# Block attention with a routed expert layer: the load order of the second and third groups of four heads

## The chip, the cores and the metric

The kernel runs on one core of a Trainium2 chip. The metric is the device time of one execution in microseconds (us). Three runs of the kernel before gave 835.05, 835.87 and 836.78 us; their median is 835.87 us. The engines are named as in the profile: PE multiplies matrices, PEld loads its weights, DVE and ACT work on vectors, POOL is the general-purpose engine, and SP only starts transfers (DMAs).

## The reference

Two parts follow each other. The first is attention for 8 batches of 8 heads, 576 positions and 64 channels per head, with a mask in blocks of 64:

```python
scores = scale * np.matmul(q, k.transpose(0, 1, 3, 2))
scores = np.where(block_i >= block_j, scores, -1000000000.0)
attn = np.exp(scores - np.max(scores, axis=-1, keepdims=True))
attn = attn / (np.sum(attn, axis=-1, keepdims=True) + 1e-09)
return np.matmul(attn, v)
```

The second takes the 4608 rows of 512 channels that this gives, picks for each row one of 8 experts by the largest of 8 logits, runs the row through two matrices of that expert with a ReLU between, and scales the result. The change touches only the first tenth of the first part.

## The kernel before, in words

**Heads and units.** Attention goes by pairs of heads: pair p = 0, 1, 2, ... is two heads, four pairs make a batch. The rows of q and k are loaded for four heads at a time, a *unit*: unit 0 is pairs 0 and 1, unit 1 (the second four heads) pairs 2 and 3, unit 2 (the third four heads) pairs 4 and 5, unit 3 pairs 6 and 7, and so on to unit 15.

**What a unit needs before its scores.** For each of k and q: a load from memory (tile `nat`, 576 KB in float32, `fetch`, line 91); a split of every value into a float16 part and the float16 rest (tile `sp`, `split`: a copy on DVE in line 96, a subtraction on POOL in line 97); a transposing DMA to a tile `tr` (`turn`, line 102; i = 0 is k, i = 1 is q). The scores multiply q by k and by a second copy of k in which the two halves of the partitions, part and rest, have changed places: the tile `sw`, made from the transposed k by two DMAs (`swap`, lines 107 and 108; this is the exchange). Lines 319 and 320 are the two score matmuls, of k and of `sw`. The pool `ld` gives `nat` four buffers and `sp` two, the number of the pool, so unit 1's first split reuses the buffer from which unit 0's k is transposed.

**Rows of v.** After the work of pair p has been written out, `load_v` (lines 303 to 306) starts four DMAs, 352 KB together, that pair's v. They are needed two pairs later, when `values` multiplies them, from line 417 on (vma and vmb first, then va and vb in lines 430 and 434).

**The order of the work.** `weave_` (line 287) goes round over generators: in each round every one of them writes out its next piece of work, first the softmax of pair p, the transposes of the probabilities of pair p - 1 (`flip`) and the products with v of pair p - 2 (`values`), then the generators in the list `later`, among them the loads. The weave of pair 0 has 5 rounds, of a later pair 8. PE follows this order exactly; on the other engines and on the SP queue a scheduler orders the instructions by priority (the order of writing) and by its own estimate of when each is ready. Every engine and the SP queue then takes its list in order, and an instruction that waits holds up all that is behind it.

**The start.** `load_start` makes unit 0 by halves: pair 0's heads through PE, the heads of pair 1 through two transposing DMAs (line 178) and two exchanges (lines 184 and 185). It makes unit 1 as well, with `nxt = Load(1)`. Its work by rounds is: round 1 of pair 0, the two transposes and unit 1's two loads; round 2, pair 1's exchange and unit 1's split of k; round 3, the transpose of unit 1's k; round 5, its split of q, which is issued after a mark `last_max` (line 363); round 1 of pair 1, the transpose of q; round 2 of pair 1, the exchange.

**The later units.** `load_heads(u)` (line 114) joins `later` at pair 2u - 3: round 1 of that pair, the two loads; rounds 5 and 6 the splits; rounds 1 and 2 of the next pair, the transposes; round 6 of it the exchange. Unit 2's loads are thus written in round 1 of pair 1, ahead of unit 1's exchange, and pair 0's v ahead of unit 1's transpose of q.

**Others.** `constants()` is written after pair 1 and is issued behind the last subtraction of a split (`last_lo`): five DMAs from POOL that set up a table of 290 KB and small weights.

Of the kernel before, what the change touches and what calls it, by code (L numbers as in the profile page):

```python
# [8 lines left out]
F16 = mybir.dt.float16  # L9
# [11 lines left out]
P = 128  # L21
# [5 lines left out]
def block_attention_top1_moe(  # L27
# [11 lines left out]
    nc = tc.nc  # L39
    B, H, S, D = q.shape  # L40
# [25 lines left out]
    MAXR = MAXH * S // P  # L66
# [8 lines left out]
    ld = tc.alloc_tile_pool(name="ld", bufs=2)  # L75
# [4 lines left out]
    class Load:  # L80
# [3 lines left out]
            self.u = u  # L84
            self.nats, self.sps, self.res = [], [], []

        def fetch(self):
            b, h0, nh = units[self.u]
            for src in (k, q):
                nat = ld.tile([P, MAXR, D], F32, name="nat", bufs=4)  # L90
                nc.sync.dma_start(nat, src[b, h0:h0 + nh].rearrange("h s d -> (h s) d").rearrange("(n p) d -> p n d", p=P))
                self.nats.append(nat)

        def split(self, i, hi, lo):
            sp = ld.tile([P, MAXR, 2, D], F16, name="sp")
            hi(sp[:, :, 0, :], self.nats[i])  # L96
            last_lo[0] = lo.tensor_tensor(sp[:, :, 1, :], self.nats[i], sp[:, :, 0, :], ALU.subtract)  # L97
            self.sps.append(sp)
# [15 lines left out]
    def load_heads(u):  # L114

        x = Load(u)
        x.fetch()
        todo = (
            lambda: x.split(0, nc.vector.tensor_copy, nc.gpsimd), lambda: x.split(1, nc.vector.tensor_copy, nc.gpsimd),
            lambda: x.turn(0), lambda: x.turn(1), x.swap,  # L120
        )
        at = 0
        for t, do in zip((4, 5, 8, 9, 13), todo):
            while at < t:
                at += 1
                yield
            do()
        x.done()

    units = [(b, h0, 4) for b in range(B) for h0 in (0, 4)]  # L130
    loaded = {}
    last_max, last_lo, last_exp = [None], [None], [None]

    def load_start():


        nr = 2 * S // P
        half = 2 * S
        nats = [ld.tile([P, 2, nr, D], F32, name="nat", bufs=4) for i in range(2)]
        sps = [ld.tile([P, 2, nr, 2, D], F16, name="sp") for i in range(2)]  # L140
        trs = [sb.tile([P, MAXR, P], F16, name=f"tr{which}") for which in (1, 0)] + [sb.tile([P, MAXH * S], F16, name="sw")]
        kT, qT = (x.rearrange("c r p -> c (r p)") for x in trs[0:2])
        sw = trs[2]
        for i in range(2):
            for src, nat in zip((k, q), nats):
                nc.sync.dma_start(
                    nat[:, i], src[0, 2 * i:2 * i + 2].rearrange("h s d -> (h s) d").rearrange("(n p) d -> p n d", p=P),
                )

        def halves(i, which, hi, lo):  # L150
            nat, sp = nats[which][:, i], sps[which][:, i]
            hi(sp[:, :, 0, :], nat)
            lo.tensor_tensor(sp[:, :, 1, :], nat, sp[:, :, 0, :], ALU.subtract)

        halves(0, 0, nc.vector.tensor_copy, nc.vector)
        halves(0, 1, nc.scalar.copy, nc.vector)
        rest = ps_t.tile([P, 512], F32, name="ps_t").rearrange("p (a n) -> p a n", n=P)
        for i, (sp, tr) in enumerate(((sps[0], kT), (sps[1], qT), (sps[0], sw))):
            sp = sp[:, 0]
            tv = tr[:, 0:half].rearrange("c (r p) -> c r p", r=nr)  # L160
            ps = ps_s.tile([P, 2, 512], F32, name="ps_s").rearrange("p a (b n) -> p (a b) n", n=P)
            for r in range(nr):
                o = ps[:, r] if r < 8 else rest[:, i]
                if i == 2:
                    for c in range(2):
                        nc.tensor.matmul(o[64 * c:64 * c + 64], sp[:, r, 1 - c, :], ident16, start=True, stop=True)
                else:
                    nc.tensor.matmul(o, sp[:, r].rearrange("p c d -> p (c d)"), ident16, start=True, stop=True)
            nc.vector.tensor_copy(tv[:, 0:4], ps[:, 0:4])
            nc.scalar.copy(tv[:, 4:8], ps[:, 4:8])  # L170
            nc.vector.tensor_copy(tv[:, 8], rest[:, i])
        loaded[0] = (qT, kT, sw)
        for which in range(2):
            halves(1, which, nc.scalar.copy, nc.gpsimd)
        yield

        for which in range(2):
            nc.sync.dma_start_transpose(
                trs[which][:, nr:], sps[which][:, 1].rearrange("p r c d -> p (r c d)")
            )  # L180
        nxt = Load(1)
        nxt.fetch()
        yield
        nc.sync.dma_start(sw[0:64, half:], kT[64:128, half:])
        nc.sync.dma_start(sw[64:128, half:], kT[0:64, half:])
        nxt.split(0, nc.vector.tensor_copy, nc.gpsimd)
        yield
        nxt.turn(0)
        yield
        yield  # L190
        with tc.issue_after(last_max[0].ins):
            nxt.split(1, nc.vector.tensor_copy, nc.gpsimd)
        yield
        nxt.turn(1)
        yield
        nxt.swap()
        nxt.done()

    with tc.high_priority(offset=3000):
        ident16 = const.tile([P, P], F16, name="ident16")  # L200
# [57 lines left out]
    with tc.manual_schedule(engines={mybir.EngineType.PE}), tc.high_priority(offset=2000):  # L258
        start = load_start()
        next(start)  # L260
# [504 lines left out]
    def split_w1(eng, b, src, c):  # L765
        sv = src.rearrange("p (g m) -> p g m", g=KF)
        split(eng, w1b[b][:, 0, c], w1b[b][:, 1, c].bitcast(BF16), sv)

    def split_w2(eng, b, src, c):
        sv = src.rearrange("p (g d) -> p g d", g=2)  # L770
        sl = slice(2 * c, 2 * c + 2)
        split(eng, w2b[b][:, 0, sl], w2b[b][:, 1, sl].bitcast(BF16), sv)
# [138 lines left out]


    loads = {2 * u - (4 if u == len(units) - 1 else 3): load_heads(u) for u in range(2, len(units))}
    loads[0] = start
    flips, prods = [], []
# [20 lines left out]
    for p in range(B * NP):  # L936
        b, hp = divmod(p, NP)
        u = p // 2
# [159 lines left out]
```

## Time and profile before

| what | value |
|---|---|
| median of three runs | 835.87 us |
| the profiled execution, its own time | 833.94 us |
| span of the trace in it | 831.9 us |
| mean granted clock of PE | 0.978 |
| PE busy | 777.9 us, 94% |
| DVE, ACT, POOL busy | 547.4, 517.4, 261.1 us |
| moved by DMAs | 151.21 MB, mean 182 GB/s |

The span runs from the first to the last instruction, so 2.0 us of the profiled execution lie outside it. In the rows, times count from the start of the span. A row of the timeline has the start, the duration, the engine, the line of the program, the operation, the tiles written and read, the number of instructions and, in brackets, the idle time before it and what ended it. For SP the duration is the time in which the queue was held by that DMA's start, not the time of the transfer. A granted clock of 1.00 is PE's upper level of 2.4 GHz, 0.50 the lower of 1.2 GHz. The share of the DMA engines can go over 1, because the packets of several transfers overlap.

### The profile page before, as it was taken

What the parts mean: (1) busy time and instruction counts of PE and PEld (TensorE: products, weight loads), DVE (VectorE), ACT (ScalarE), POOL (GpSimd) and SP (SyncE); (2) the same over time, 40 slices, a digit from 0 to 9 for tenths busy, and PEclk for the clock granted to TensorE, in tenths of its full rate; (3) what the DMA queues carried; (4) which work ended last, traced back from release to release, by engine and by line L of the source; (5) the groups of instructions that cost most, each with busy time, mean ns of one, the idle gap of its engine ahead of it and who ended that gap; (6) DMA issues with size and microseconds to landing.
All of it is one profiled execution on the core that took longest, in us unless ns stands there. A gap on an engine that the chain in (4) does not pass through costs nothing. (4 is left out here: it accounts for less than half of the span.)

```text
span 831.9 us, 17237 instructions
## 1 busy us (share of the span) xinstructions
PE 777.9 (94%) x6214; PEld 523.5 (63%) x6238; DVE 547.4 (66%) x1188; ACT 517.4 (62%) x1210; POOL 261.1 (31%) x233
## 2 busy tenths in 40 slices
PE   5599999999999999889996999999999999999995
PEld 3366666666676666555673766676656666776652
DVE  6467777878687777758561766786567656786540
ACT  4478786877778777666312855775555555775530
POOL 4322142424232243473236462223123222300001
PEclk9699999999999999999999999999999999999998
DMA  8999889799999899983158499685789968822611
GB/s 156 199 179 171 185 153 194 153 188 191 183 201 175 181 184 200 183 268 107 33 165 208 119 316 303 209 236 114 235 268 290 292 182 210 234 48 57 220 40 41
DMA packets 267053, 151.21 MB, mean 182 GB/s; under 512 B 235600, under 2 KB 235664, under 8 KB 266960
## 3 DMA queue, kind: packets, MB, share of 16 engines
q1 hardware_dynamic: 258688, 130.74, 68.6%
q0 software_dynamic: 8272, 19.29, 7.8%
q8 instruction: 51, 0.84, 0.4%
q14 instruction: 42, 0.34, 0.2%
HBM read 124.33 MB, written 19.73 MB: 173 GB/s over the span
## 5 line engine op out<-in xcount | busy, mean ns | idle before, releaser
L873 PEld LDWEIGHTS <-w1b 128*128 128x128 f16 (+1 forms) x2112 | 184.0, 98 | 26.5 <-issue 3.2
L873 PE MATMUL ps_s<-xt,w1b 128*128 128x256 f16 (+3 forms) x1824 | 182.1, 261 | 0.5 <-DVE w1b L763 0.4
L334 ACT ACTIVATE pt<-ps_s,nbs 128x448 f32<-128x448 f32 (+1 forms) x314 | 163.8, 531 | 23.9 <-DVE nbs L327 10.0
L900 PE MATMUL ps_t<-w2b,hh 128*128 128x512 f16 (+1 forms) x584 | 175.8, 379 | 2.3 <-ACT hh L881 2.3
L763 DVE TENSOR_TENSOR w2b<-w2f,w2b 128x1024 bf16<-128x1024 f32 x76 | 88.0, 1221 | 114.2 <-ACT w2b L762 114.2
L410 ACT COPY pT<-ps_t 128x512 f32<-128x512 f32 (+3 forms) x221 | 97.8, 463 | 74.1 <-PE ps_t L402 73.1
L402 PE MATMUL ps_t<-ident,pt 128*128 128x128 f32 (+1 forms) x800 | 133.0, 287 | 2.5 <-DVE xn L459 2.4
L900 PE MATMUL ps_t<-w2b,hl 128*128 128x512 f16 x304 | 115.2, 379 | 1.7 <-DVE hl L882 0.6
L97 POOL TENSOR_TENSOR sp<-nat,sp 128x1152 f16<-128x1152 f32 x30 | 71.2, 2375 | 145.1 <-DVE sp L96 111.2
L903 ACT ACTIVATE ys<-ps_t,ids 128x512 f32<-128x512 f32 x38 | 26.0, 688 | 137.7 <-PE ps_t L900 91.5
L319 PE MATMUL ps_s<-tr,tr 128*128 128x448 f16 (+1 forms) x378 | 99.6, 286 | 6.4 <-ACT pt L334 6.0
L900 PEld LDWEIGHTS <-hh 128*128 128x128 f16 x608 | 59.2, 98 | 69.2 <-ACT hh L881 2.8
L904 POOL DMA_INDIRECT out_dram<-ys,ids x38 | 43.4, 1143 | 185.2 <-ACT ys L903 134.5
L320 PE MATMUL ps_s<-sw,tr 128*128 128x448 f16 (+1 forms) x378 | 92.2, 286 | 9.4 <-DMA sw<-tr 9.4
L402 PEld LDWEIGHTS ps_t<-ident,pt 128*128 128x128 f32 (+1 forms) x800 | 87.8, 143 | 18.4 <-issue 5.5
L763 DVE TENSOR_TENSOR w1b<-w1f,w1b 128x1024 bf16<-128x1024 f32 x76 | 88.0, 1221 | 0.2 <-ACT w1b L762 0.2
L434 PE MATMUL ps_a<-pT,vb 128*64 128x512 f32 (+3 forms) x256 | 83.5, 450 | 0.0
L430 PE MATMUL ps_a<-pT,va 128*64 128x512 f32 (+3 forms) x256 | 83.5, 450 | 0.0
L372 DVE TENSOR_REDUCE nmx<-ps_s 128x2 f32<-128x896 f32 (+1 forms) x63 | 60.2, 956 | 32.7 <-PE ps_s L322 32.5
L762 ACT CAST w1b<-w1f 128x1024 f16<-128x1024 f32 x76 | 74.0, 1044 | 0.3 <-DMA w1f<-in_moe_w_dram 0.2
L762 ACT CAST w2b<-w2f 128x1024 f16<-128x1024 f32 x76 | 73.6, 1042 | 0.0
L736 POOL DMA_INDIRECT xg<-x_d,ids x38 | 55.3, 1455 | 53.5 <-DMA ids<-tab_d 20.6
(196 smaller groups left out, 1122.0 us busy)
## 6 DMA issues: line engine op xcount, KB each, us to landing
w1f<-in_moe_w_dram SPq DMA_DIRECT2D x76, 512.0 KB
w2f<-in_moe_w_dram SPq DMA_DIRECT2D x76, 512.0 KB
nat<-in_k_dram SPq DMA_DIRECT2D x15, 576.0 KB
nat<-in_q_dram SPq DMA_DIRECT2D x15, 576.0 KB
sw<-tr SPq DMA_DIRECT2D x30, 288.0 KB
x_d<-xn SPq DMA_DIRECT2D x32, 256.0 KB
va<-in_v_dram SPq DMA_DIRECT2D x32, 128.0 KB
vb<-in_v_dram SPq DMA_DIRECT2D x32, 128.0 KB
```

What stands on the lines that cost most here:

```text
L97: last_lo[0] = lo.tensor_tensor(sp[:, :, 1, :], self.nats[i], sp[:, :, 0, :], ALU.subtract)
L319: nc.tensor.matmul(ps_ap, qq, k1[ab][:, c0:c1], start=True, stop=False)
L320: nc.tensor.matmul(ps_ap, qq, k2[ab][:, c0:c1], start=False, stop=last)
L334: last_exp[0] = nc.scalar.activation(probs[t][0:r, ab * n:(ab + 1) * n], ap, AF.Exp, bias=nbs[0:r, t, ab:ab + 1], scale=SCALE, accum_out=s ...
L402: nc.tensor.transpose(ps[:, i, 0:rows], probs[t][0:rows, P * col:P * col + P], ident[0:rows, 0:rows])
L410: copies[next(nth)](pT[:, r:r + m, Q0[t]:Q0[t] + rows], ps[:, i:i + m, 0:rows])
L430: nc.tensor.matmul(pa[0:64, P * j:512], va[:, j, :], pT[:, 1 + 2 * j, 64 + P * j:576], start=False, stop=(j == 3),)
L434: nc.tensor.matmul(pa[64:128, P * j:512], vb[:, j, :], pT[:, 2 + 2 * j, 64 + P * j:576], start=False, stop=(j == 3),)
L762: nc.scalar.copy(hi, src)
L763: eng.tensor_tensor(lo, src, hi, ALU.subtract)
L873: nc.tensor.matmul(ph[:, f4].rearrange("p (h n) -> p h n", n=P), wv[:, cc, f, :], xv[:, cc], start=(k == 0), stop=(k == 3 * KD - 1))
L900: nc.tensor.matmul(py, hv[:, f, h], wv[:, f, :], start=(k == 0), stop=(k == 3 * KF - 1))
```

## The change: the diff

```diff
-        def fetch(self):
+        def fetch(self, *which):
             b, h0, nh = units[self.u]
-            for src in (k, q):
+            for src in [(k, q)[w] for w in which or (0, 1)]:
...
         def split(self, i, hi, lo):
-            sp = ld.tile([P, MAXR, 2, D], F16, name="sp")
+            sp = ld.tile([P, MAXR, 2, D], F16, name="sp", bufs=4)
...
     def load_heads(u):
 
         x = Load(u)
+        late = LATE if u == 2 else 0
+        for i in range(late):
+            yield
         x.fetch()
...
+    LATE = 4
...
-        sps = [ld.tile([P, 2, nr, 2, D], F16, name="sp") for i in range(2)]
+        sps = [ld.tile([P, 2, nr, 2, D], F16, name="sp", bufs=4) for i in range(2)]
...
+
+        nxt = Load(1)
+        nxt.fetch(0)
...
-        nxt = Load(1)
-        nxt.fetch()
+        nxt.fetch(1)
+        nxt.split(0, nc.vector.tensor_copy, nc.gpsimd)
         yield
         nc.sync.dma_start(sw[0:64, half:], kT[64:128, half:])
         nc.sync.dma_start(sw[64:128, half:], kT[0:64, half:])
-        nxt.split(0, nc.vector.tensor_copy, nc.gpsimd)
-        yield
         nxt.turn(0)
         yield
         yield
...
             nxt.split(1, nc.vector.tensor_copy, nc.gpsimd)
         yield
         nxt.turn(1)
-        yield
         nxt.swap()
         nxt.done()
+
 
```

Unit 1's work by rounds becomes: its load of k is written right behind unit 0's loads, ahead of pair 0; round 1 of pair 0, the load of q and the split of k; round 2, the transpose of k; round 4, the split of q; round 5, the transpose of q and the exchange. All of it is then written in pair 0's weave, ahead of pair 0's v and of pair 1. Unit 2 alone moves by four rounds: its loads to round 5 of pair 1, its splits to rounds 1 and 2 of pair 2, its transposes to rounds 5 and 6 of pair 2, and its exchange from round 6 of pair 2 to round 2 of pair 3, behind pair 2's v and behind the loads of unit 3, which stay in round 1 of pair 3. `sp` has four buffers. No instruction is added or taken away. Since `last_lo` is then unit 1's last subtraction when `constants()` is written, those five DMAs wait for that one and no longer for unit 2's.

## Rows read from the trace of the kernel before

**Rows 1.** Waits of PE, whole run: line, releaser: us in total, times, longest.

```profile
PE ps_s L320 <- DMA sw<-tr: 9.4, 2, 8.7
```

**Rows 2.** Timeline of PE: first scores of pairs 1 to 4, first of L417.

```profile
19.83 0.19 PE L319 MATMUL ps_s<-tr,tr 128*128 128x64 f16 x1
...
30.72 0.20 PE L319 MATMUL ps_s<-tr,tr 128*128 128x64 f16 x1
39.60 0.23 PE L320 MATMUL ps_s<-sw,tr 128*128 128x64 f16 x1 [8.68 <-DMA sw<-tr]
...
41.75 0.37 PE L417 MATMUL ps_t<-pT,vma 128*64 128x64 f32 x1
...
51.48 0.19 PE L319 MATMUL ps_s<-tr,tr 128*128 128x64 f16 x1
...
61.50 0.19 PE L319 MATMUL ps_s<-tr,tr 128*128 128x64 f16 x1
```

**Rows 3.** Timeline of the SP queue from 14 to 54 us.

```profile
14.57 0.59 SPq L185 DMA_DIRECT2D sw<-tr  x1
20.09 2.68 SPq L102 DMA_TRANSPOSE tr<-sp  x1
22.81 0.58 SPq L303 DMA_DIRECT2D va<-in_v_dram  x1
...
25.97 2.76 SPq L102 DMA_TRANSPOSE tr<-sp  x1
28.77 0.57 SPq L91 DMA_DIRECT2D nat<-in_k_dram  x1
...
31.54 2.35 SPq L107 DMA_DIRECT2D sw<-tr  x1
...
46.04 0.52 SPq L107 DMA_DIRECT2D sw<-tr  x1
...
51.61 1.64 SPq L91 DMA_DIRECT2D nat<-in_q_dram  x1
```

**Rows 4.** Stretches: length, busy us of PE, PEld, DVE, ACT, POOL, granted clock, DMA share, GB/s.

```profile
17.00:21.00 4.00, 1.85 (x16) 1.29 (x15) 3.97 (x7) 2.67 (x8) 2.61 (x2) 0.86 0.05 12
21.00:26.00 5.00, 4.54 (x19) 2.81 (x20) 2.99 (x12) 3.54 (x15) 2.12 (x1) 0.50 0.95 184
26.00:27.00 1.00, 1.00 (x7) 0.90 (x6) 0.62 (x1) 0.40 (x2) 0.00 (x0) 0.63 0.28 54
...
39.60:43.60 4.00, 4.00 (x27) 3.26 (x27) 1.68 (x8) 1.60 (x9) 4.00 (x6) 0.50 1.10 230
39.00:58.00 19.00, 18.40 (x142) 12.17 (x142) 11.35 (x34) 12.83 (x47) 4.92 (x6) 0.87 1.08 205
...
53.00:57.00 4.00, 4.00 (x38) 2.82 (x36) 2.77 (x8) 3.56 (x17) 0.00 (x0) 1.00 1.27 243
57.00:60.00 3.00, 3.00 (x25) 1.57 (x20) 2.14 (x7) 2.45 (x8) 1.92 (x1) 1.00 0.74 151
60.00:61.00 1.00, 1.00 (x11) 0.59 (x10) 0.65 (x2) 1.00 (x4) 0.46 (x1) 1.00 0.00 1
```

**Rows 5.** Timeline of DVE and POOL: the splits of units 1 and 2, the table.

```profile
16.81 0.75 DVE L96 CAST sp<-nat 128x1152 f16<-128x1152 f32 x1
...
18.49 2.19 DVE L96 CAST sp<-nat 128x1152 f16<-128x1152 f32 x1
...
34.17 0.76 DVE L96 CAST sp<-nat 128x1152 f16<-128x1152 f32 x1 [3.06 <-DMA nat<-in_k_dram]
37.49 0.76 DVE L96 CAST sp<-nat 128x1152 f16<-128x1152 f32 x1 [2.56 <-DMA nat<-in_q_dram]
...
17.70 2.37 POOL L97 TENSOR_TENSOR sp<-nat,sp 128x1152 f16<-128x1152 f32 x1 [6.82 <-DVE nbs L327]
20.75 2.36 POOL L97 TENSOR_TENSOR sp<-nat,sp 128x1152 f16<-128x1152 f32 x1 [0.69 <-DVE sp L96]
...
40.63 0.74 POOL L267 DMA_DIRECT2D tab_d<-tinit  x1
```

## The prediction

> **What bounds the kernel now.** I read the waits of PE first, since it is busy for 94% of the span. Over the whole run its largest releaser is the exchange, 9.4 us, of which one wait has 8.7 [rows 1]. The timeline of PE gives its place: the first score of pair 2 against k runs at 30.72, its partner against `sw` at 39.60, and PE stands for 8.68 us between [rows 2]. So pair 1 takes 10.89 us from its first score (19.83 to 30.72), pair 2 takes 20.76 with the wait, pair 3 takes 10.02 (51.48 to 61.50).
>
> The SP queue, read next, tells why the exchange is late. Unit 1's k is transposed at 20.09. Then come pair 0's v, the transpose of q at 25.97, unit 2's loads from 28.77, and at 31.54 at last the exchange [rows 3]. It does not need the transposed q, nor the v, nor the loads; it stands behind them. Its transfer also runs behind theirs: the DVE copy of unit 2's q starts at 37.49 as soon as that load has landed [rows 5], and PE is released 2.1 us later [rows 2].
>
> The stretches show the second thing to see: the DMA engines have little room here. Between 39 and 58 us they move 205 GB/s at a share of 1.08; they stand almost still from 17 to 21 (12 GB/s), when SP waits for unit 1's first split, dip from 26 to 27 (54 GB/s), and run dry only at 60 [rows 4]. Whatever is moved forward pushes something else back.
>
> **The change part by part.**
>
> *Removed: the wait of 8.68 us.* In the new order the exchange of unit 1 follows its two transposes with only those ahead. When can they go? SP is free for the transpose of k at 15.2 (14.57 + 0.59 [rows 3]). It needs the split. The copy took 0.75 us at 16.81 and the subtraction 2.37 us at 17.70 [rows 5]; no row shows when the load of k had landed. Bounds: the copy cannot come later than now by this edit, and if it goes one round up, into the softmax of the first rows, it is done some 2 to 4 us earlier. I take 3, a subtraction ending at 17 rather than 20.07, because the queue's transfers end at 17 in any case and nothing else wants the engines then [rows 4]. So the transpose of k moves from 21.3 (its transfers begin 1.2 us after 20.09) to about 17.7.
>
> The copy of q stands at 18.49 and took 2.19 us beside POOL's subtraction, against 0.75 for the same shape at other times; POOL began q at 20.75 and took 2.36 [rows 5]. With k's subtraction gone earlier I take the short value: the copy ends near 19.2, the subtraction near 21.6, and the transpose of q starts there instead of at 25.97. The bounds are 20.5 and 23.1 (20.75 + 2.36, nothing gained). It holds SP for 2.76 us; the exchange, with 2.1 us of transfer behind the transpose's, lands between 27.5 and 30.5. Pair 2 wants it at 30.72, or up to 1.5 us sooner if pairs 0 and 1 run shorter. The wait goes, or leaves less than 1 us.
>
> *Removed with it: a cold start.* PE is at the lower clock after the wait, 0.50 from 39.6 to 43.6 [rows 4]. From the release, pair 2 needs 11.88 us (39.60 to 51.48), pair 3 10.02 [rows 2], so 1.86 us are the clock. If nothing took their place, the two would give 8.68 + 1.86 = 10.54 us, and pair 4 would start at 50.96 instead of 61.50.
>
> *Moved back: pair 0's v.* Four DMAs now follow the exchange and are issued by 28. Line 417 first reads them 2.15 us after pair 2's restart at 39.60 [rows 2], so near 32. They have 352 KB, 1.7 us at 205 GB/s; cover 0 to 2 us, cost taken as nothing, up to 1 us if the exchange lands at 30.5.
>
> *Moved forward: the table and small weights of `constants()`.* POOL starts them at 40.63 [rows 5]; they move to behind q's subtraction, near 22. Some 0.3 MB, 1.6 us of transfer at 205 GB/s, can fall between the transposes and the exchange. They lie inside the margin just given, and leave a later stretch, so no cost in sum.
>
> *Moved back: unit 2, by four rounds.* This decides the size. In pair 2 DVE meets unit 2's copies in rounds 1 and 2, and everything behind a copy waits for its load. Before, both copies waited, 3.06 and 2.56 us [rows 5], while PE stood still anyway; that cover is gone. More, unit 2's exchange now stands behind unit 3's loads, just as unit 1's did behind unit 2's.
>
> Take the list of transfers from unit 1's transpose of k to the end of unit 3's loads. In both orders it has the same members, except that unit 2's exchange now comes last (it was issued at 46.04, ahead of unit 3's loads, whose second started at 51.61 [rows 3]). Before, the list ran from 21.3 to about 57.5: from 57 to 60 there were 453 KB, 352 of them pair 3's v, so 100 KB of loads were left at 57 [rows 4]. After: it begins 3.6 us earlier (17.7), has a new gap between the transposes of k and q, since v no longer fills the wait for q's split (17.7 + 2.7 = 20.4 to 22.8, 2.4 us), and loses the old gaps at 26 and 52, about 1.8 together. End: 57.5 - 3.6 + 2.4 - 1.8 = 54.5, and with 0.5 us for the landing unit 2's exchange is there at 55.0. Pair 4 would be ready at 50.96. So some 4 us come back, spread over DVE's waits for the loads of units 2 and 3 and PE's for this exchange; they are one delay, not to be added up, since all hang on the same list.
>
> *Sum.* Pair 4 starts at 55.0 instead of 61.50: 6.5 us. If the new waits are long enough to take PE to the lower clock, 1.86 us go again; between 0 and 1.86 I take 0.9. Gain 5.6 us. Ends: the list may end 2 us sooner or later by the bounds on the two splits and the gap, and the clock 0.9 either way, so 2.7 to 8.5. From 60 us on the engines run dry at times [rows 4], so the order behind is set by the rounds and moves along.
>
> *At nothing:* the argument of `fetch` (no instruction), the load of k written earlier (it is ahead of unit 0's transposes on SP already), and two more `sp` buffers, memory alone beside what they free.
>
> Against the profiled execution: 833.94 - 5.6 = 828.3. The median stood 1.93 above it, so 835.87 - 5.6 = 830.3.
>
> **The rivals.**
>
> *The queue keeps up.* Plain loads went at 243 GB/s from 53 to 57 against the mean of 205 [rows 4]. If the list went at 243, its 34.4 busy us (21.3 to 57.5 less 1.8) would shrink to 29.0, and from 17.7 with the gap of 2.4 it would end at 49.1; pair 4 would not wait. Then the gain is 10.5, with 0.7 more if the short copy of q also shortens pair 0: 835.87 - 11 = 824.9. Against it stand the transposes and the v, at 184 [rows 4]. A sentence for the page: the Trainium skill (DMA: Bandwidth & Descriptors, section on bandwidth) gives 341 GB/s for a load of 1 MB, which would make the same case more strongly; the rows here stay well under it.
>
> *The exchange is not ahead.* The scheduler decides the SP queue, not the writing alone. If unit 2's loads still go first, or unit 1's q is not split sooner, the wait stays: 835.9, no change. Against it: in the rows the queue follows the order of writing for v, transposes, loads and exchange.
>
> *Slower: the four rounds.* If unit 2's loads are held until round 5 of pair 1 in fact, and the engines are idle meanwhile, four rounds (5.0 us at 10.02 for eight) are added to the list: it ends at 62.5, the exchange lands at 63.0, pair 4 starts 1.5 us later than at 61.50, cold for 1.86 more: 835.87 + 3.4 = 839.3. It decides once unit 2's first load is issued 4 us or more after the present 28.77, with the engines standing idle between. For it: the rounds are counted in PE's time. Against it: by round 5 of pair 1 SP is still busy with v, so the queue should not be empty.
>
> **How the numbers follow.** A measurement of this kernel can tell about 0.2% from no change, 1.7 us. Chances: the forecast 0.58, the queue keeps up 0.23, not ahead 0.10, slower 0.09. The first two are faster by more than 1.7 us: 0.81; 0.10 the same, 0.09 slower. The forecast's own range is 835.87 less 8.5 and less 2.7, 827.4 to 833.2; to reach the first rival the low end goes to 824.3, and the high end to 834.2, the edge of no change.
>
> **What would show each step.** Right: no wait of PE on `sw` near 31; the two transposes of unit 1 and the exchange ahead of line 303 on SP; transfers from 17 or 18 us on; pair 2 starting at 29 to 31 at the full clock; waits of DVE line 96 in pairs 2 and 3, and unit 2's exchange issued behind unit 3's loads, with PE waiting for it at 52 to 56. Wrong: pair 4 starting at 51 with no wait (too little gain forecast), a wait at line 417 for v, or an idle stretch of the DMA engines before unit 2's loads.

## The result, and the profile after

The changed kernel took 841.41 us in the median of 7 runs (839.80 to 846.97), the kernel before 836.20 us in 7 runs beside them: a ratio of 1.0067, 95% interval 1.0041 to 1.0093. The change costs 5 us; 830.3 had been forecast, with 824.3 to 834.2 as the range. The profiled execution of the changed kernel took 841.41 us itself, with a span of 839.4 us. Two executions of later kernels, of 1003.53 and 1650.32 us, are slow ones and stand in no median or ratio below. In the changed kernel the lines up to 108 keep their numbers, and those behind are 3 to 7 higher: L319 and L320 are L324 and L325, L303 is L308, L417 is L422.

The waits of PE over the whole run come first again:

```profile
PE ps_s L325 <- DMA sw<-tr: 10.9, 4, 8.3
PE ps_t L422 <- DMA vma<-in_v_dram: 4.1, 2, 2.7
```

The exchange still costs PE 10.9 us, where it cost 9.4 [rows 1]. The timeline of PE shows that the long wait has only moved, from pair 2 to pair 4:

```profile
30.45 0.20 PE L324 MATMUL ps_s<-tr,tr 128*128 128x64 f16 x1 [1.21 <-DMA tr<-sp]
32.58 0.20 PE L325 MATMUL ps_s<-sw,tr 128*128 128x64 f16 x1 [1.93 <-DMA sw<-tr]
...
44.81 0.19 PE L324 MATMUL ps_s<-tr,tr 128*128 128x64 f16 x1
...
54.83 0.19 PE L324 MATMUL ps_s<-tr,tr 128*128 128x64 f16 x1
63.28 0.23 PE L325 MATMUL ps_s<-sw,tr 128*128 128x64 f16 x1 [8.26 <-DMA sw<-tr]
```

Pair 2 waits 1.21 + 1.93 us instead of 8.68 and starts 7 us sooner [rows 2]. But from its release at 32.58 to pair 3's first score at 44.81 it takes 12.23 us, where it took 11.88 with the lower clock before and pair 3 takes 10.02. Pair 4 stands from 55.0 to 63.28, later than its start at 61.50 before. The SP queue tells what is ahead of its exchange:

```profile
15.78 10.58 SPq L102 DMA_TRANSPOSE tr<-sp  x2
26.45 0.54 SPq L107 DMA_DIRECT2D sw<-tr  x1
27.68 1.01 SPq L308 DMA_DIRECT2D va<-in_v_dram  x1
...
31.54 0.59 SPq L91 DMA_DIRECT2D nat<-in_k_dram  x1
...
37.92 0.62 SPq L311 DMA_DIRECT2D vmb<-in_v_dram  x1
43.32 6.99 SPq L102 DMA_TRANSPOSE tr<-sp  x2
...
53.51 1.55 SPq L91 DMA_DIRECT2D nat<-in_q_dram  x1
55.18 2.63 SPq L107 DMA_DIRECT2D sw<-tr  x1
```

Unit 1's exchange is now ahead of v and of unit 2's loads, as planned. Between pair 1's v (issued by 38.54) and unit 2's transposes at 43.32 SP issues nothing, and unit 2's exchange stands at 55.18 behind unit 3's loads. The splits say why SP waits; they come from the timelines of DVE and POOL:

```profile
40.03 0.75 DVE L96 CAST sp<-nat 128x1152 f16<-128x1152 f32 x1
43.72 0.75 DVE L96 CAST sp<-nat 128x1152 f16<-128x1152 f32 x1
```

```profile
21.20 0.74 POOL L272 DMA_DIRECT2D tab_d<-tinit  x1
40.92 2.37 POOL L97 TENSOR_TENSOR sp<-nat,sp 128x1152 f16<-128x1152 f32 x1 [16.43 <-DVE nbs L332]
```

Unit 2's split of k begins at 40.03 and ends on POOL at 43.29; the transpose follows 0.03 us later. The two copies show no wait for a load, unlike before [rows 5]: they stand late in DVE's own list, k's behind the third group of pair 2's maxima (line 377 at 39.02), q's behind the last one (line 388 at 43.05). The stretches of 1 us give the DMA engines' side (columns as in [rows 4]):

```profile
24.00:25.00 1.00, 1.00 (x10) 0.72 (x9) 0.48 (x4) 0.98 (x3) 0.50 (x1) 1.00 1.08 69
25.00:26.00 1.00, 0.59 (x5) 0.28 (x4) 0.97 (x2) 1.00 (x6) 0.00 (x0) 1.00 2.09 50
...
35.00:36.00 1.00, 1.00 (x8) 1.00 (x5) 0.20 (x1) 0.66 (x5) 0.00 (x0) 0.50 1.22 202
...
40.00:41.00 1.00, 1.00 (x8) 0.16 (x4) 0.91 (x4) 0.57 (x3) 0.08 (x1) 1.00 0.08 13
41.00:42.00 1.00, 1.00 (x11) 0.72 (x10) 0.23 (x1) 1.00 (x3) 1.00 (x1) 1.00 0.00 0
...
44.00:45.00 1.00, 1.00 (x16) 0.82 (x13) 0.54 (x2) 0.77 (x3) 0.45 (x1) 1.00 0.47 95
...
64.00:65.00 1.00, 1.00 (x6) 0.69 (x5) 0.59 (x2) 0.00 (x0) 0.11 (x1) 0.50 1.20 233
```

Three things are to be read here. The engines stand still from 40 to 44.4. From 24 to 26, while what POOL has started from 21.20 on (the table and the small weights) is on its way, they are busy by their share (1.08 and 2.09) and move only 69 and 50 GB/s. And PE is at its lower clock after the new wait, as it was after the old one [rows 4], and at 34 to 37 after the short waits of pair 2 as well.

One measure compares all kernels below: the start of a pair's first maximum on DVE, the first thing done with its scores. The table, worked out from the timelines of DVE, gives it as the difference in us to the profile of before, whose pair 2 stands at 40.73, pair 4 at 62.57 and pair 5 at 72.64. Pairs count from 0; minus is sooner.

| kernel | 2 | 4 | 5 | 7 | 16 | 25 |
|---|---|---|---|---|---|---|
| before, second profile | +1.1 | +1.1 | +1.1 | +1.0 | +1.1 | +1.2 |
| changed | -7.5 | +1.8 | +3.5 | +3.5 | +5.2 | +5.1 |
| table late | -10.4 | -0.9 | +1.2 | +1.2 | +3.0 | +3.0 |
| copies sooner, again | -8.1 | 0.0 | +1.8 | +1.8 | +3.5 | +2.9 |
| both together | -10.3 | -1.7 | +0.7 | +0.7 | +4.3 | +4.2 |
| changed, a third time | -7.4 | +2.8 | +4.6 | +4.6 | +7.2 | +6.4 |
| exchange first | -8.1 | -6.4 | -6.0 | -5.7 | +5.4 | +4.3 |
| unit 3 later | -8.3 | -3.7 | -2.3 | -2.9 | +12.2 | +11.2 |
| no late | -9.2 | -5.1 | -3.5 | -2.7 | +10.3 | +9.4 |
| exchange order alone, again | -9.5 | -9.2 | -7.2 | -7.2 | +7.0 | +6.1 |
| four buffers, again | -3.5 | -3.0 | -3.0 | -3.0 | -3.9 | -3.7 |

The loss of the changed kernel is made at pairs 4 and 5: +3.5 there, of which 1.6 between the two pairs are put down to the lower clock. Other profiles of the same kernel have +4.6 and, below, +1.5 at pair 5. Another 1.7 us come by pair 16. Between pair 25 and the end of the span the difference goes from 5.1 to 7.5 us, about as far as the two profiles of before drift apart there (from 1.2 to 3.0 us at pair 30).

### The profile page after: what moved, and what is told of

Same layout as the page of the kernel before. It is cut to its first block, busy times and chain, and to the rows that moved or that the text cites. A ratio compares the mean times of both kernels' runs of the same rounds, so it can differ in the third digit from the quotient of the medians.

```text
span 839.4 us, 17223 instructions
## 1 busy us (share of the span) xinstructions
PE 781.1 (93%) x6214; PEld 524.9 (63%) x6238; DVE 545.4 (65%) x1188; ACT 517.9 (62%) x1210; POOL 262.9 (31%) x233
## 5 line engine op out<-in xcount | busy, mean ns | idle before, releaser
L324 PE MATMUL ps_s<-tr,tr 128*128 128x448 f16 (+1 forms) x378 | 100.2, 287 | 5.4 <-ACT pt L339 3.8
L909 POOL DMA_INDIRECT out_dram<-ys,ids x38 | 49.0, 1291 | 178.4 <-ACT ys L908 103.9
L325 PE MATMUL ps_s<-sw,tr 128*128 128x448 f16 (+1 forms) x378 | 92.5, 286 | 10.9 <-DMA sw<-tr 10.9
L388 DVE TENSOR_REDUCE nmx<-ps_s 128x1 f32<-128x576 f32 x64 | 48.3, 755 | 38.4 <-PE ps_s L327 37.6
```

Source lines behind the costliest of these rows:

```text
L324: nc.tensor.matmul(ps_ap, qq, k1[ab][:, c0:c1], start=True, stop=False)
L325: nc.tensor.matmul(ps_ap, qq, k2[ab][:, c0:c1], start=False, stop=last)
```

## The experiments

My theory after the result: unit 2's exchange is late by its place behind unit 3's loads, and that list of transfers ends 8 us later than forecast because the DMA engines stand still while unit 2 is split, and because the table's transfers run beside unit 1's transposes. The rivals: the four rounds delay the loads of unit 2, or the place in the queue is no matter.

**Exchange first.** The changed kernel, with unit 2's exchange written in the round of its transpose of q, ahead of pair 2's v and of unit 3's loads.

```diff
-        for t, do in zip((4, 5, 8, 9, 13), todo):
+        for t, do in zip((4, 5, 8, 9, 9 if u == 2 else 13), todo):
```

> Edit: in the changed kernel, unit 2's exchange is written right behind its transpose of q, so that it stands ahead of pair 2's v and of unit 3's loads. Theory A (order alone: pair 4 waits 8.3 us because the exchange stands behind the loads): the wait of PE on sw near 55 goes to under 1 us, the first max of pair 4 comes near 56 instead of 64.4, the time falls by about 10 us to 831. Rival B (the list of transfers is late as a whole, and DVE takes its copies in order): unit 3's loads now land later, near 57 and 59.5, the DVE copies of unit 3 hold up pair 3's last maxima and pair 4's first until 60 to 61; the wait on sw goes, but the time falls by only 3 to 4 us, to 837 or 838, about that of the kernel before.

Measured: 845.47 us, ratio 1.0133 [1.0091, 1.0174]. The exchange is issued at 50.58 and the wait is gone:

```profile
55.48 0.20 PE L325 MATMUL ps_s<-sw,tr 128*128 128x64 f16 x1 [0.37 <-DMA sw<-tr]
```

The place in the queue decides the wait; of 8.26 us, 0.37 are left. But the time is no better; neither expectation had one so long. The lead of 6 us holds to pair 7 and is lost from pair 8 to 16 (table). Moving this one DMA also changes the lists of the later batches, since the scheduler orders everything behind anew: PE's list differs from before's near 94, 141 and 186 us, where the transposes of a finished batch stand between the scores, and is the same there in the changed kernel. So this run shows what the wait hangs on, and not what it is worth.

**Table late.** The changed kernel with `constants()` written one pair later.

```diff
-    CP = 1
+    CP = 2
```

> Edit: in the changed kernel, constants() (the table of 290 KB and the small weights, five DMAs from POOL) is written after pair 2 and not after pair 1, so that it is issued behind unit 2's last subtraction and no longer at 21 us beside unit 1's transpose of q. Theory A (the table's DMAs slow that transpose; 69, 50 and 103 GB/s from 24 to 27 us): PE's waits at the start of pair 2, 1.2 and 1.9 us, shrink to under 1 us in all, pair 2 starts 2 to 3 us sooner; pair 4 gains at most as much, the time falls by 0 to 2 us. Rival B (the transpose of q is slow by itself): pair 2 still waits about 3 us, and the time stays at 841.

Measured: 843.22 us, ratio 1.0067 [1.0041, 1.0094]. SP's queue in this run:

```profile
15.23 8.16 SPq L102 DMA_TRANSPOSE tr<-sp  x2
```

The two transposes are done on SP 8.16 us after the first is issued, instead of 10.58. In the other profiles with the table at 21 to 22 us it is 9.4 to 10.2, in the other two with a late table 8.2 and 8.4; so the table beside unit 1 costs 1.1 to 2.4 us at that place. Pair 2 starts with a wait of 0.29 us and keeps the full clock (1.00 from 26 to 52), and unit 2's copy of k, behind the same maxima in DVE's list, starts at 35.10 instead of 40.03. The only list that differs from the changed kernel's is POOL's. Pair 4 comes 2.7 us sooner, and 2.2 of that are left at pair 16; but with the table at 41.94 a like hole appears at 45 to 47, and pair 4 still waits 9.43 us, until 60.55. The ratio is the one that the changed kernel had in its own comparison, so a gain in time is not shown.

**No late.** The changed kernel with unit 2 in its old rounds.

```diff
-    LATE = 4
+    LATE = 0
```

> Edit: LATE = 0 in the changed kernel, unit 2's loads, splits, transposes and exchange at their old rounds. On SP and DVE this gives the same order as the kernel with the exchange written first; only the table differs, which is issued behind unit 2's subtractions. Theory A (the four rounds are what loses): the exchange of unit 2 is ahead of unit 3's loads, no wait on sw at pair 4, and without the table at 21 us pair 2 starts 2 to 3 us sooner; 829 to 834, faster than the kernel before. Rival B (the copies of units 2 and 3 on DVE wait for their loads, whatever the rounds say): DVE waits of 5 us and more in pairs 2 and 3, pair 4's first max at 59 to 61, 834 to 838.

Measured: 844.07 us, ratio 1.0085 [1.0055, 1.0116]. Unit 2's loads are issued at 28.78, behind unit 1's exchange and pair 0's v as in the changed kernel, and its transposes at 42.17 (43.32 there). The run above, with a late table too but the late rounds, has the loads at 28.73 and the transposes at 38.39. So the late rounds hold back neither: the loads follow SP's queue, and the transposes wait for the split of k, whose copy starts at 38.88 here. The idle stretch before them is there with the old rounds too (0.02 and then 0.00 of the engines from 39 to 43). What the rounds do change is the place of the exchange, which is now ahead of unit 3's loads, and pair 4 waits 1.55 us for it (and 1.08 for the transposed q and k). Both expectations had a shorter time; the lead of 5.1 us at pair 4 goes as with exchange first, and PE's list differs from before's at the same three places.

**Buffers alone.** The kernel before with four split buffers in both places, and no other edit.

```diff
-            sp = ld.tile([P, MAXR, 2, D], F16, name="sp")
+            sp = ld.tile([P, MAXR, 2, D], F16, name="sp", bufs=4)
...
-        sps = [ld.tile([P, 2, nr, 2, D], F16, name="sp") for i in range(2)]
+        sps = [ld.tile([P, 2, nr, 2, D], F16, name="sp", bufs=4) for i in range(2)]
```

> Edit: the kernel before with four sp buffers, nothing else of the change. Theory A (the order of the queue holds the exchange back, not the buffers): unit 1's k is split and transposed some 4 to 5 us sooner, but its exchange still stands behind pair 0's v, the transpose of q and unit 2's loads; PE waits 6 to 8.7 us for it, the time stays within 2 us of the kernel before, 834 to 836. Rival B (the buffers by themselves cost time later on, by other places in memory or other orders): 838 or more.

Measured: 832.71 us, ratio 0.9958 [0.9932, 0.9985]: faster than before, by more than either expectation had. DVE's copy of unit 1's k starts at 11.60 instead of 16.81 [rows 5], its transpose at 15.26 instead of 20.09, the exchange at 27.88 instead of 31.54 [rows 3], and PE waits 7.28 us instead of 8.68. So the copy had been held by the buffer, not by its place in the order, and all lists but DVE's stay as they were.

**Copies sooner.** The changed kernel, with both of unit 2's copies one maximum sooner in DVE's list.

```diff
+            with tc.issue_after(copied[2, 0].ins) if b == 0 and hp == t == 2 else nullcontext():
...
+            with tc.issue_after(copied[2, 1].ins) if b == 0 and hp == 2 else nullcontext():
```

> Edit: in the changed kernel, unit 2's two copies stand sooner in DVE's list: k's behind pair 2's second maximum and no longer its third, q's behind the third and no longer the fourth. Nothing else moves in the SP queue. Theory A (the DMA engines stand idle from 40 to 44 us because these copies come late in DVE's list, and the whole list of transfers behind them is late by that): the transposes of unit 2 are issued from 41.7 and 44.2 us instead of 43.3 and 46.9, the exchange of unit 2 lands 2 to 3 us sooner, pair 4's first maximum comes at 61.5 to 62.5 instead of 64.4; the time falls by about 2 us. Rival B (the rate of the transfers alone decides, a gap here only moves the wait): pair 4's first maximum stays at 64 or later.

Measured: 858.45 us, ratio 0.9987 [0.9963, 1.0010], on a chip where the kernel before took 859.66. Its traces show stalls of about 4 to 5 us that the profile puts down to a releaser named remote, in every kernel on that chip; one of them lay in pair 2 of this profile, and the copies ran at 42.12 and 43.89, later than in the changed kernel. Inconclusive; repeated below.

**Exchange order alone.** The kernel before with four buffers, and unit 1's exchange written in the round of its transpose of q.

```diff
         nxt.turn(1)
-        yield
         nxt.swap()
         nxt.done()
+        yield
```

> Edit: the kernel before with four sp buffers and the exchange of unit 1 written in the round of its transpose of q, so that it is ahead of unit 2's loads on SP; pair 0's v stays ahead of the transpose of q, LATE is not there. Theory A (an earlier start is given back later, because the lists of DVE, ACT and SP that the scheduler then makes for the batches behind are worse ones, as when the exchange of unit 2 was put first): pair 2 starts near 30, pair 4's first maximum at 55 to 58, 4 to 6 us ahead of the kernel before until pair 7, then 2 to 3 us are lost on each unit up to pair 17; the time is 838 to 846. Rival B (what is lost later is the work of the change's other parts, the late unit 2 and the v behind the exchange): the lead stays, 829 to 832.

Measured on the same chip: 858.53 us, ratio 0.9969 [0.9941, 0.9996]. Pair 2 waits 0.82 us and pair 4 is 9.2 us ahead of the first profile of before, of which nothing is left by pair 12. Held against the kernel before on its own chip (next), which has the stalls too, the lead is 10.8 us at pair 4 and 4.6 at pair 12. What the stalls do to either was not separated, so this was repeated too.

**Changed and before, again,** on that chip, one run each, no edit.

> The changed kernel once more, for a second trace: how much of its distance to the kernel before comes in the same place. If the lists decide, pair 5 is again 3 to 4 us behind the kernel before, with PE's wait of about 8 us on unit 2's exchange; if it is scatter, that wait differs by more than 2 us.

> The kernel before once more, for a second trace: the scatter of its pairs 10 to 30. If the drift of 4 us that the changed kernel shows there against the first trace is scatter of the runs, this trace also differs from the first by 2 to 4 us there; if it is the lists, this trace stays within 1 us of the first.

Measured: 854.6 and 860.91 us. The waits come back as they were: 8.90 us at pair 4 in the changed kernel, 8.66 at pair 2 in the one before, and pair 5's first maximum is at 74.18 and 74.16. The changed kernel was expected 3 to 4 us behind there and is level, since unit 2's transposes were issued at 40.94 in this profile and its wait ended at 61.54. So the place of the loss comes back, its size does not. Behind pair 8 the stalls named remote come in; two single runs with such stalls tell nothing of a difference under 1%.

**Both together.** Copies sooner and the table late, on another chip, where the kernel before took 836.62 us.

```diff
-    CP = 1
+    CP = 2
...
+            with tc.issue_after(copied[2, 0].ins) if b == 0 and hp == t == 2 else nullcontext():
...
+            with tc.issue_after(copied[2, 1].ins) if b == 0 and hp == 2 else nullcontext():
```

> The changed kernel with two of its side effects taken out: the table's DMAs go one batch part later, and DVE's copies of the third four heads stand one and two maxima earlier in its list. Theory B (the forecast's list is right and only its two neglected terms, the idle gap from 40 to 44.4 and the table beside unit 1's transposes, spoil it): SP holds the two transposes of unit 1 for about 8.2 us instead of 10.6, the idle stretch before unit 2's transposes shrinks from 4.4 to under 2.5, and PE's wait at pair 4 ends at 56 to 59 instead of 63.28; pair 4's first maximum at -3 to -6 against before. Rival (the queue order alone decides, unit 2's exchange behind unit 3's loads): the wait still ends at 61 or later. Time: by Theory B 829 to 835 if the lead is kept; if later batches give it back as in the run with the exchange first, 835 to 843 with the lead at pair 4 all the same.

Measured: 840.51 us, ratio 1.0041 [1.0023, 1.0059]. PE at pair 4:

```profile
59.72 0.23 PE L325 MATMUL ps_s<-sw,tr 128*128 128x64 f16 x1 [7.54 <-DMA sw<-tr]
```

The exchange lands 3.6 us sooner than in the changed kernel (63.28), and 4.5 sooner than in the changed kernel on this chip (64.24, below). It was expected between 56 and 59, the rival had 61 or later; neither came. The transposes of unit 1 take 8.23 us on SP. The stretches show how much of the idle time is left, and the table's hole at its new place:

```profile
37.00:38.00 1.00, 0.44 (x3) 0.20 (x3) 1.00 (x3) 1.00 (x5) 1.00 (x1) 1.00 0.00 0
38.00:39.00 1.00, 1.00 (x10) 0.73 (x9) 1.00 (x1) 0.78 (x4) 0.52 (x1) 1.00 0.00 0
39.00:40.00 1.00, 1.00 (x12) 0.75 (x12) 1.00 (x3) 0.57 (x2) 0.79 (x1) 1.00 0.22 46
44.00:45.00 1.00, 1.00 (x14) 0.68 (x9) 0.21 (x1) 1.00 (x7) 0.83 (x2) 1.00 2.59 155
45.00:46.00 1.00, 1.00 (x10) 0.78 (x9) 0.80 (x1) 0.59 (x3) 0.00 (x0) 1.00 0.06 6
```

Both terms are real, but neither was taken out whole. The idle time fell from 4.4 to about 3 us, where under 2.5 was expected: copy, subtraction and transpose of unit 2 are a chain, and nothing else is on the queue meanwhile. And the table's hole now stands between unit 2's transposes and its exchange, still ahead of that exchange.

**Copies sooner, again,** the same kernel as above, one run.

> The copies-sooner kernel once more, because a stall of 3.9 us named remote fell into pair 2 in its first profile. Theory: the copies start at 37 to 39 instead of 40.03 and 43.72, the transposes of unit 2 are issued by 41.5, the idle stretch is under 3 us, and PE's wait at pair 4 ends 1.5 to 3 us sooner than 63.28, at 60 to 62. Rival (the copies are not what the transposes wait for): the transposes are issued at 43 or later and the wait ends at 63 as in the changed kernel.

Measured: 836.06 us in that run. The copies start at 38.58 and 40.35, the transposes at 41.86, the engines stand still for about 3 us until 43.06, and the wait of 5.99 us ends at 61.49: as the theory had it, though q's copy and the transposes came a little later than expected and the idle time is not clearly under 3 us.

**Buffers alone, again,** with more runs.

> Four split buffers in the kernel of before and nothing else, again, with more rounds: a gain of 2 to 4 us (0.9958 before, interval 0.9932 to 0.9985). Rival (the first result was the chip's scatter): a ratio within 0.998 and 1.002.

Measured: 834.38 us, ratio 0.9981 [0.9958, 1.0004]. The gain is at the lower end of what was expected, and this interval just reaches no change. The trace is 3 to 4 us ahead from pair 2 to 25; in the first run with these buffers it was 1.5 to 2.7.

**Changed, a third time,** beside these.

> The changed kernel again beside the others: PE's wait at pair 4 is 8 to 9 us, and its time is 0.3 to 0.9% above before's, as in the recorded comparison; rival (the sign hangs on the chip): within 0.3% of before or below it.

Measured: 844.42 us, ratio 1.0086 [1.0058, 1.0114]; the wait at pair 4 is 8.43 us. Against it, both together is 4.5 us sooner at pair 4 (60.85 to 65.36) and 3.9 us shorter in time. The lists of PE and SP are the same in these two, and those of DVE, ACT and POOL differ in the first batch alone: here, where the lists stay, a shorter wait is worth about what it is shorter. It is one comparison, and in the traces 2.2 of the 4.5 us are left at pair 25.

Still open then was why the kernels without the wait end no earlier. Three more runs went to that, beside a kernel before of 835.77 us.

**Before, a second profile.**

> The kernel before once more, for a second profile to hold the others against. Theory (the loss of 3 us between pairs 26 and 28, seen in every kernel, is a lucky stretch of the first profile): this profile shows the same loss there and its pairs 28 to 32 come 2 to 4 us later than in the first, while pairs 2 to 16 agree within 0.7 us. Rival (the loss belongs to the changed kernels): it agrees with the first profile within 1 us all along.

Measured: 834.91 us. It stands 1.0 to 1.2 us behind the first profile from pair 2 to 25, from a wait of 9.51 us at pair 2, and 3.0 behind at pair 30. A miss of 0.4 us on the first half of the expectation. Of the 3.8 us that the changed kernel loses from pair 25 to 28, 2.0 are then the luck of the first profile.

**Unit 3 later.** The changed kernel with the loads of unit 3 two rounds later, behind unit 2's exchange.

```diff
-        late = LATE if u == 2 else 0
+        late = LATE if u == 2 else 2 if u == 3 else 0
```

> The changed kernel with the loads of the fourth four heads two rounds later, so that the exchange of the third four heads is ahead of them on SP. Theory A (the wait at pair 4 is the place in the queue): the exchange is issued at about 52, PE's wait there is under 1 us, pair 4's first maximum 6 to 9 us ahead of the changed kernel's 64.41, at 55.5 to 58. Rival (the idle stretch alone makes it late): the wait stays over 4 us. For the time: if the lead at pair 4 is worth its length, 829 to 834; if the later batches give it back, as in the run with the exchange first, 836 to 846, with the loss between pairs 7 and 16.

Measured: 844.03 us in the median of three runs (843.90 to 851.19), ratio 1.0143 [1.0075, 1.0211]; with so few runs the size of the loss is rough. The exchange is issued at 52.74; PE waits 3.07 us at 57.90, more than the 1 us expected, because the exchange now comes 2.2 us later than with exchange first. Pair 4 is 5.6 us ahead of the changed kernel, a little less than the 6 to 9 expected. The lead goes after pair 7, as with exchange first; the wait can thus be taken away from either side, with the same end.

**Exchange order alone, again.**

> Four split buffers and the exchange of the second four heads one place further up in the kernel of before, again on another chip. Theory (the wait goes, and the later batches' lists give the lead back): pair 2 waits under 1 us, pairs 3 to 7 are 8 to 12 us ahead of before, and the lead is gone by pair 12; time within 0.5% of before. Rival (the giving back was the remote stalls of that chip): the lead holds to pair 32 at 6 us or more, and the time is 826 to 832.

Measured: 841.32 us in the median of five runs, ratio 1.0074 [1.0048, 1.0100], over the 0.5% expected. The rival falls: the lead of 7 to 9 us is lost on this chip too, with no stall named remote. So it is in every kernel here in which the long wait is gone: exchange first, no late, unit 3 later and this one lose 11 to 15 us against before from pair 7 to 16, and PE's list differs from before's at the same three places in all of them. The kernels of the table that keep PE's list lose 3.7 us there at most. PE's wait for v grows:

```profile
PE ps_t L417 <- DMA vma<-in_v_dram: 13.3, 5, 5.1
PE ps_t L524 <- ACT pT L410: 5.0, 6, 1.7
```

In the second profile of before the first of these is 4.6 us in 2 waits. One of the new ones is at 119.37, 5.06 us. The stretch of 11 us ahead of it, here and then in the second profile of before:

```profile
108.00:119.00 11.00, 6.23 (x53) 3.73 (x49) 5.81 (x17) 7.03 (x26) 5.64 (x4) 0.99 1.41 74
```

```profile
108.00:119.00 11.00, 10.84 (x99) 7.21 (x97) 8.53 (x25) 9.30 (x31) 7.65 (x7) 1.00 0.64 100
```

POOL's five indirect writes into the table for this batch start at 102.27 here and at 108.14 before, and the DMA engines are busier (share 1.41 against 0.64) for fewer bytes; the `vma` that PE waits for had been issued at 106.37, 13 us earlier. So the lists of a batch's end, ordered anew, put the table's writes ahead of a v that is due, where before they came behind it. I read this at one place, and that the new order makes the loss is argued from the lists and not shown: no run holds the later lists fixed while the wait is taken away, so what that alone would give stays open.

## Why the prediction was wrong

*Read rightly.* What bounds the kernel; that unit 1's exchange goes ahead and pair 2's wait nearly goes; that unit 2's exchange stands behind unit 3's loads and comes last. The landing of unit 1's exchange was given as 27.5 to 30.5; it was at 32.58, and with the table late at 29.60. The size of a cold start, 1.86 us, came out as 1.6 at pair 4.

*The step that failed first* is the list of transfers: "End: 57.5 - 3.6 + 2.4 - 1.8 = 54.5, and with 0.5 us for the landing unit 2's exchange is there at 55.0". It landed at 63.28. The list was summed as if it ran through, with one gap for unit 1's split of q. Unit 2 has the same chain of load, copy, subtraction and transpose, and the engines stand for 4.4 us while it runs. From the start of k's copy to the first transfers of the transposes it is 4.5 us in the changed kernel (40.03 to 44.5), with the table late (35.10 to 39.6) and with copies sooner (38.58 to 43.06). Before, the copy began 5.4 us after its load was issued (28.77 to 34.17 [rows 3], [rows 5]), and unit 1's exchange and pair 1's v ran beside the chain. Now it begins 8.5 us after it (31.54 to 40.03), behind pair 2's maxima, when pair 1's v is nearly through; and the exchange is no cover any more, since it has gone ahead. By the difference some 3 of the 4.4 us are the copy's place, an estimate; copies sooner took some 1.3 of them back. I had costed the copies by their waits for the loads; those waits did not come, the copies themselves came late.

The landing behind the list was mis-sized too. DVE's copy of unit 3's q starts at 60.91 in the changed kernel, and PE is released 2.4 us later. In its third profile that copy waits for the load itself, and PE is released at 64.24, 2.6 us later:

```profile
61.66 0.76 DVE L96 CAST sp<-nat 128x1152 f16<-128x1152 f32 x1 [2.37 <-DMA nat<-in_q_dram]
```

The prediction had read 2.1 us for the same thing at unit 1, and took 0.5 here.

*The second* is the table, "so no cost in sum". Its bytes were priced at 205 GB/s, 1.6 us inside a margin. Its transfers make the queue's slow for 2.4 us in this profile (10.58 less 8.16; 1.1 to 2.4 over all profiles), at a place where the exchange was due. Idle time, table and landing, 4.4 + 2.4 + 1.9 (2.4 less 0.5), make 8.7 us against the 8.3 between 55.0 and 63.28. That is an addition and not a run: both together brought the exchange 3.6 to 4.5 us sooner, and 59.72 is still 4.7 behind 55.0.

*Hidden by this* is "Removed with it: a cold start". It was not removed: after waits of 1.21 and 1.93 us pair 2 ran at 0.50 from 34 to 37 and took 12.23 us, so pair 4 was ready at 54.83 and not at 50.96. With the exchange there at 55.0 this would not have shown in the time. There is also a slip in the sum: a subtraction ending 3.07 us sooner does not move the transpose by 3.6. In fact it ended at 14.77, 5.3 us sooner, and SP took the transpose as soon as it was free, at 15.78.

*The third* is the last sentence of the sum, that from 60 us on the order "is set by the rounds and moves along". It does not: leads of 3.7 to 9.2 us at pair 4 are lost by pair 16 in four kernels, and the changed kernel falls back by 1.7 us from pair 5 to 16. An edit of the first batch changes the scheduler's lists of the later ones; in the changed kernel too, where PE's list is before's, SP's is in another order near 96, 146 and 192 us.

*The rival that came nearest* is the slower one: exchange at 63.0, cold, 839.3 us. Its time was nearly right by luck, for the mechanism was another. I had looked for an empty queue ahead of unit 2's loads and argued against it, "by round 5 of pair 1 SP is still busy with v"; SP was busy there indeed, and the loads wait for it in the old rounds too. The empty stretch lies behind them, between load and transpose, and stays with the old rounds. I gave this rival 0.09 and no price to the place that decided.

*The buffers* were put at nothing, "memory alone beside what they free", and what they free was counted with the rounds. They are the one part with a gain of its own, 0.2 and 0.4% in two comparisons, of which one is clear of no change: the copy of unit 1's k had been waiting for a buffer, PE's and SP's lists stay as they were, and the lead holds from pair 2 to 25. Of all versions here, before with these alone is the one that came out ahead of before twice.

## What to carry to other kernels

When transfers are moved forward, redraw the queue after the move and ask of each chain of load, split and transpose what else is on the queue while it runs: a transfer that was late may have been the cover of the next chain, and a wait that goes may let other work stand ahead of that chain's first step. Price small transfers by a stretch in which they ran, not by their bytes. And in a scheduled program compare the order of every queue to the end before the lead of the first pairs is booked as a gain.

## What was unexpected of the hardware

*Small transfers from POOL can slow the others.* With the table started at 21 to 22 us, unit 1's two transposes took 9.4 to 10.6 us on SP, with a late table 8.2 to 8.4. Behind the table's start a stretch has a share of about 2 or more, and there or next to it few bytes: 50 GB/s at 2.09 in the changed kernel, 155 at 2.59 and then 6 at 0.06 in both together. In the kernel before, where POOL starts it at 40.63, no stretch of 1 us from 40 to 48 has a share over 1.29 or moves under 122 GB/s. What makes the difference, no run showed.

*A copy beside a subtraction waits it out.* With copies sooner, DVE's copy took 2.10 us beside POOL's subtraction, against 0.75 alone, as once before [rows 5]. It ended 0.6 us after POOL in three cases: 20.68 after 20.07, 39.13 after 38.52, 42.45 after 41.83. The Trainium skill (SBUF — State Buffer, section "SBUF: two separate sides") has DVE and POOL share one pair of ports, which the first to start holds for its whole instruction, if DVE's is of a kind that uses the pair; the three ends agree with that.

*Chips differ by more than the change.* The kernel before took 836 us on three chips and 859.66 on one, with stalls of up to 5 us, in most of its traces about once a batch, that no trace from the other chips has. What they are, no run showed.
